# A linear attention and a feed-forward layer on one core: the turn of batch 2's queries behind the load of its values, and the work around tile 0's second layer placed anew

## The chip, the core and the metric

The kernel runs on one core of a Trainium2 chip. The metric is the device time of one execution in microseconds (us); a time given for a kernel is the median of several executions. The engines are named as the profile names them: PE multiplies matrices (PEld is its loading of weights), DVE is the vector engine, ACT the scalar engine, POOL and SP issue most of the transfers (DMAs). PE writes its results to banks of the memory PSUM; all other tiles lie in SBUF.

## The reference

Eight batches of eight heads, 576 rows of 64 numbers each, are put through attention without a softmax; the heads of a row are joined to 512 numbers, and the 4608 rows go through a layer of 2048 hidden units.

```python
kv  = einsum('bhsd,bhse->bhde', k, v)
out = einsum('bhsd,bhde->bhse', q, kv)
rms = sqrt(mean(out * out, axis=-1, keepdims=True) + 1e-06)
x   = (out / rms * g_norm)          # heads joined: [4608, 512]
h   = x @ w_in                      # [512, 2048]
g   = h * (1 / (1 + exp(-1.702 * h)))
y   = g @ w_out                     # [2048, 512]
```

## The kernel before

The rows are worked off in nine tiles of 512: tile t holds the first 512 rows of batch t, and tile 8 the 64 rows that each batch leaves over. A tile has a first layer (h and its gate) and a second layer (the product with w_out). Tile 0 multiplies plainly: 64 products of 128x512 in the first layer (`first_columns`, L473) and 64 in the second (`project_all`, L819). From tile 1 on both layers use seven block products in place of eight (`SevenIn`, L584, and `Seven`, L704), which need sums of blocks: of w_in (`w_in_sums`, L495 to L498), of w_out (`weight_sum`, L612, into `tw`), of the tile's x (`Sums.form`, L512) and of the gated units (`Seven.sums`, L636).

While PE works on a tile, the attention of the next batches is pushed in between. This order is written out by hand: `at1(i, ...)` puts a unit of work behind step i of a tile's first layer, `at2(n, ...)` behind product n of its second. For a batch the units are `kv` (products of k and v into the PSUM tile `kvp`, L259 or L247, then copies into `kvb` or `kvd`), `out` (products with the turned q, L302, and squares on ACT, L320), `ss` (a product with ones, L379, and the reciprocal root on ACT, L381) and `apply` (outT times rs into xT, DVE, L393). From batch 2 on `rows` (L332), `add_up`, `roots` and `turn` stand in their place, and the queries are turned by a transposing DMA from SP (`transpose_q`, L290, into `qTd`; `transpose_rest`, L294, into `qTr`).

Every engine works its own list in order and waits for semaphores, and so do the queues from which DMAs are issued. Nearly all loads are issued by POOL, in one list: batch 0's q, k, v, w_in, then w_out between batch 1's q, k, v (`early_load`, L91; the last pieces of k and v hold the channels of heads 4 to 7), then batch 2's q (`load_q`), and its k and v (`load_kv`, L115, with L120 for the rows left over), which go into the buffers that batch 1's k and v lay in. w_in comes in pieces: hidden blocks 0 to 3 in four pieces of 128 rows, with blocks 8 and 9 ahead of the fourth, then the others; tile 0's hidden blocks are computed in the order `COLS`, which begins 0, 1, 2, 3, 8, 9.

At the start `busy(n)` lets PE multiply zeros n times (128x512, into a bank that nobody reads, L867): 12 before the first turn of q, and 2 in each of two later places.

PSUM has three rings of banks: `ps_a` (three, tag att), `ps_h` (three, tag hT) and `ps_o` (two). A new tile of a ring waits until the readers of the tile three (or two) before it have ended.

Of the kernel before, what the change touches and what calls it, by code (L numbers as in the profile page):

```python
# [16 lines left out]
def kernel(  # L17
# [10 lines left out]
    nc = tc.nc  # L28

    B, H, S, D = q.shape  # L30
# [47 lines left out]
    HF, HN = FO // 2, DM // 2  # L78
# [8 lines left out]
    def early_src(n, b, c0, c1):  # L87
        return srcs[n][b, 2 * c0 : 2 * c1].rearrange("h (p j) d -> p h (j d)", j=NJ)

    def early_load(n, b, c0, c1):  # L90
        nc.gpsimd.dma_start(  # L91
            out=raw[n][0:PE_, c0:c1, :].rearrange("p c (l x) -> p (c l) x", l=2),
            in_=early_src(n, b, c0, c1),
        )
# [13 lines left out]
    kv_rows = {n: raw[n].rearrange("p c x -> p (c x)") for n in "kv"}  # L108
    RW = J * D
    RS = H * RW  # L110
# [26 lines left out]
    def q_rows(b):  # L137

        rows = qbuf if b % 2 else qraw.rearrange("p c x -> p (c x)")
        return rows[:, 0 : H * J * D]  # L140
# [14 lines left out]
    for n in "kqv":  # L155
# [11 lines left out]
        out=ident,  # L167
        in_=ident,
# [36 lines left out]
    def load_w_out(f0, f1):  # L205
        nc.gpsimd.dma_start(
            out=w_out_sb[:, f0:f1, :],
            in_=moe_w_out[f0 * P : f1 * P, :].rearrange("(fo ki) n -> ki fo n", ki=P),
        )
# [11 lines left out]
    class Attention:  # L221
        ss_pool = rest_pool = (ps_a, "att")
# [62 lines left out]
                    r = slice(hl * D, (hl + 1) * D)  # L285
                    copy(self.engine, self.kb[to, c0:c1, half, 1 - hl], self.kvp[r, c0:c1, :])

        def transpose_q(self):
            self.qTd = attn.tile([P, H * J // 2, P], F16, name="qTd", tag="qTd", bufs=1)
            nc.sync.dma_start_transpose(out=self.qTd, in_=q_rows(self.b))  # L290

        def transpose_rest(self):
# [123 lines left out]
    class First(Early):  # L416


        ss_pool = (ps_o, "o")
# [23 lines left out]
    class Second(Early):  # L443


        ss_pool = rest_pool = (ps_h, "hT")
# [82 lines left out]
    def copy(engine, to, src):  # L529
        (nc.vector.tensor_copy if engine == "D" else nc.scalar.copy)(to, src)  # L530
# [280 lines left out]
    def project_all(gT, units):  # L811

        os = {}

        def project(mo, fo):
            if fo == 0:
                pool, tag = (ps_h, "hT") if mo < 2 else (ps_o, "o")
                os[mo] = pool.tile([P, DM], F32, name="o", tag=tag)
            nc.tensor.matmul(  # L819
                os[mo],  # L820
                gT[:, fo, mo * P : (mo + 1) * P],
                w_out_sb[:, fo, :],
                start=(fo == 0),
                stop=(fo == FO - 1),
            )
            if fo == FO - 1:
                copy = nc.scalar.copy if mo % 2 else nc.vector.tensor_copy
                copy(osbs[0][:, mo, :], os[mo])

        steps = [(mo, 4 * i + k) for i in range(3) for mo in range(4) for k in range(4)]  # L830
        steps += [(mo, f + k) for f in (12, 14) for mo in range(2) for k in range(2)]
        steps += [(mo, 12 + k) for mo in (2, 3) for k in range(4)]
        for n, (mo, fo) in enumerate(steps):
            project(mo, fo)
            for u in units.get(n, ()):
                u()
# [28 lines left out]
    def busy(n):  # L865
        for _ in range(n):
            nc.tensor.matmul(  # L867
                idle_ps,
                kvb[1][:, 0, :],
                kvb[1].rearrange("p c r -> p (c r)"),  # L870
                start=True,
                stop=True,
            )
# [15 lines left out]
    a0.ss(0)  # L889
    a0.out(1)  # L890
    a0.q(2)
    a0.kv(2)
    a0.ss(1)
    a0.apply(0)
# [1 line left out]
    a0.q(3)  # L896
    a0.apply(1)
    d0 = Hidden(0)
    a0.kv(3)
    a0.ss(2)  # L900
    a0.apply(2)
# [22 lines left out]
    load_w_out(8, 10)  # L924
    load_w_out(10, 12)
    early_load("v", 1, 0, 2)
    load_w_out(12, 14)
    early_load("k", 1, 2, NPAIR)
    early_load("v", 1, 2, NPAIR)
    load_w_out(14, FO)  # L930

    made = {}
# [44 lines left out]
    live = {0: a0}  # L977
# [4 lines left out]
    for t in range(NT):  # L982
        b = t + 1
        u1, u2 = {}, {}

        def at1(i, f, *args):
            u1.setdefault(i, []).append(lambda: f(*args))

        def at2(i, f, *args):
            u2.setdefault(i, []).append(lambda: f(*args))  # L990

        def of(b, name, *args):
            return lambda: getattr(live[b], name)(*args)

        if t == 0:
            for l in range(2):
                at1(6, nc.vector.memset, kvd[l], 0.0)
            at1(7, of(0, "out", NPAIR))
            at1(7, scale_w_in, 0, 4)
            at1(7, w_in_sums, 0, 2)  # L1000
            at1(8, start, 1)
            at1(12, scale_w_in, 4, 6)
            at1(12, w_in_sums, 2, 3)
            at1(13, load_q, 2)
            at2(4, setattr, a0, "ss_pool", Attention.ss_pool)
            at2(4, of(0, "ss", NPAIR, True))
            at2(4, of(0, "apply", NPAIR))
            at2(18, weight_sum, 0, 0, HF)
            at2(18, scale_w_in, 6, 8)
            at2(18, w_in_sums, 3, 4)  # L1010
            for c in range(NPAIR):
                at1(12, of(1, "pack_q", c))
                at2(9 + 3 * c, of(1, "q", c))
                at2((36, 36, 49, 49)[c], of(1, "kv", c))
                at2((41, 43, 54, 55)[c], of(1, "out", c))
                at2((45, 50, 58, 60)[c], of(1, "ss", c))
                at2((48, 52, 58, 62)[c], of(1, "apply", c))
            for n in range(1, 4):
                at2(19, weight_sum, n, 0, 4)
                at2(38, weight_sum, n, 4, 6)  # L1020
            at2(39, load_kv, 2, 0, H // 2, False)
            at2(51, clear_rest)
            at2(51, load_kv, 2, H // 2, H)

            def first_sum():
                made[1] = Sums(1, xT[1])
                made[1].form(0)

            at2(55, first_sum)
        elif b < B:  # L1030
            todo = plan(t)
            at = todo.attn
            if t == 1:
                at1(todo.steps.index("kv"), of(b, "kv_all", "D"))
                at1(5, start, b)
                at1(5, of(b, "transpose_q"))
                at1(5, of(b, "transpose_rest"))
                at1(4, nc.scalar.preload_act_table_set, "gelu_apprx_sigmoid_and_others")
                for n, i in ((1, 8), (2, 11), (3, 16)):
                    at1(i, weight_sum, n, 6, HF)  # L1040
                at1(22, load_kv, 3)
                at1(22, load_q, 3)
                at2(88, start, 3)
                at2(88, of(3, "kv_all", "A"))
                at2(89, load_kv, 4)
                at2(89, load_q, 4)
            elif t + 2 < B:
                at2(at["rows"][0], start, t + 2)
                at2(at["rows"][0], of(t + 2, "kv_products"))
                at2(52, of(t + 2, "kv_copies", "A"))  # L1050
                if t + 3 < B:
                    at2(at["rows"][0], load_kv, t + 3, 0, H, False, "k")
                    at2(101, after_turn, b)
                    at2(101, load_kv, t + 3, 0, H, True, "v")
                    at2(101, after_queries, t + 2)
                    at2(101, load_q, t + 3)
            if t + 2 < B:
                at2(49 if t > 1 else 100, of(t + 2, "transpose_q"))
                at2(100, of(t + 2, "transpose_rest"))
            at2(at["table"], nc.scalar.preload_act_table_set, "abs_reciprocal_sqrt_and_small")  # L1060
            for h in range(2):
                at2(at["roots"][h], of(b, "roots", h))
            for j in range(J):
                if j < J // 2:
                    at2(at["rows"][j], of(b, "rows", j))
                for name in ("add_up", "turn"):
                    at2(at[name][j], of(b, name, j))
            rest = (80, 90, 96, 97) if 1 < t < B - 2 else (46, 74, 80, 82)
            at2(rest[0], of(b, "out", NPAIR))
            at2(rest[1], of(b, "ss", NPAIR))  # L1070
            at2(rest[2], of(b, "apply", NPAIR))
            at2(rest[3], nc.scalar.preload_act_table_set, "gelu_apprx_sigmoid_and_others")
        elif t < B:
            for name in ("ss_pool", "rest_pool"):
                at2(16, setattr, live[1], name, (ps_a, "att"))
            at2(16, of(1, "out", NPAIR))
            at2(34, nc.scalar.preload_act_table_set, "abs_reciprocal_sqrt_and_small")
            at2(44, of(1, "ss", NPAIR))
            at2(50, of(1, "apply", NPAIR))
            at2(52, nc.scalar.preload_act_table_set, "gelu_apprx_sigmoid_and_others")  # L1080
        layers(t, u1, u2)
# [30 lines left out]
```

## Time and profile before

| | |
|---|---|
| median of 3 runs | 259.14 us (258.35, 259.14, 259.88) |
| the profiled execution, its own time | 259.74 us |
| its span, from first to last instruction | 258.0 us |
| PE busy | 251.7 us (98%) |
| DVE, ACT, POOL busy | 193.9, 177.1, 57.0 us |
| mean granted clock of PE | 0.993 |

The profile is of one execution. A window is a stretch of the span in us from its start; `PEclk` is the share of the full clock that PE was granted in it. In a row of the timeline the first number is the start, the second the time until the last of the group has ended; what ended an idle time stands in brackets. For a DMA the row of the queue gives when it was issued, and the row of the issues how long it took from issue to landing.

### The profile page before, as it was taken

How to read it: one execution, taken by the hardware profiler on the slowest of the kernel's cores; microseconds unless marked ns; L12 is line 12 of the kernel's file. 1: busy time of each engine (PE TensorE's matmuls, PEld its weight loads, DVE VectorE, ACT ScalarE, POOL GpSimd, SP SyncE). 2: the span in 40 equal slices, each digit the busy share in tenths (PEclk: the TensorE clock that was granted, in tenths of full speed). 3: DMA queues.
4: the chain of work that ended last, by engine and by line, in shares of the span. 5: the costliest groups of instructions: out<-in, count | busy, mean ns of one | idle time of the engine just before them, and what ended most of it. 6: DMA issues, size and time to landing. Idle time of an engine off the chain costs nothing.

```text
span 258.0 us, 6355 instructions
## 1 busy us (share of the span) xinstructions
PE 251.7 (98%) x2596; PEld 204.4 (79%) x2596; DVE 193.9 (75%) x344; ACT 177.1 (69%) x322; POOL 57.0 (22%) x92
## 2 busy tenths in 40 slices
PE   8899999999999999999999999999999999999994
PEld 2444454788888888888888888898888888888883
DVE  1546685899958986798679867987799787857872
ACT  3458743988758894899579957995799469536800
POOL 8773244208061013301150134000000000000013
PEclk9979999999999999999999999999999999999999
DMA  7999999999989979996999699909500430012005
GB/s 181 194 188 206 204 204 197 216 216 115 184 159 208 221 91 224 153 158 81 186 184 164 84 205 135 190 5 136 202 4 0 84 163 3 0 57 108 3 19 145
DMA packets 68687, 35.33 MB, mean 137 GB/s; under 512 B 37970, under 2 KB 66258, under 8 KB 68402
## 3 DMA queue, kind: packets, MB, share of 16 engines
q0 software_dynamic: 37632, 18.31, 55.3%
q1 hardware_dynamic: 30624, 16.29, 27.4%
q8 instruction: 20, 0.33, 0.5%
q10 hardware_dynamic: 402, 0.33, 0.5%
q14 instruction: 9, 0.07, 0.1%
HBM read 36.70 MB, written 9.44 MB: 179 GB/s over the span
## 4 chain that ended last, share of the span: by engine, by line
PE 93%; DMA 4%; issue 0%; POOL 0%; DVE 0%
PE o L704 38%; PE h L584 38%; PE hT L473 6%; PE o L819 5%; DMA vbuf<-in_v_dram 2%; DMA qraw<-in_q_dram 2%; PE kvp L247 2%; PE outR L332 1%; PE ss L379 1%; PE outT L302 1%; PE q L454 0%; PE kvp L259 0%; PE outT L306 0%; PE kv L259 0%; DVE osb L684 0%
## 5 line engine op out<-in xcount | busy, mean ns | idle before, releaser
L561 ACT ACTIVATE gT<-h 128x512 f16<-128x512 f32 x96 | 52.5, 601 | 5.6 <-PE h L584 5.6
L584 PEld LDWEIGHTS <-ws 128*128 128x128 f16 x512 | 50.1, 98 | 5.9
L704 PEld LDWEIGHTS <-gS 128*128 128x128 f16 x512 | 49.1, 98 | 6.1 <-DVE gS L636 0.3
L584 PE MATMUL h<-xS,ws 128*128 128x256 f16 x384 | 52.2, 273 | 0.0
L704 PE MATMUL o<-tw,gS 128*128 128x256 f16 x384 | 45.6, 273 | 0.0
L584 PEld LDWEIGHTS <-w_in_sb 128*128 128x128 f16 x384 | 37.4, 98 | 4.7
L704 PEld LDWEIGHTS <-gT 128*128 128x128 f16 x384 | 37.6, 98 | 4.3
L704 PE MATMUL o<-w_out_sb,gT 128*128 128x256 f16 x256 | 31.4, 273 | 0.0
L584 PE MATMUL h<-xT,w_in_sb 128*128 128x256 f16 x224 | 31.1, 272 | 0.0
L681 DVE TENSOR_TENSOR osb<-o,qf 128x512 f32<-128x512 f32 (+1 forms) x25 | 16.7, 669 | 11.7 <-PE o L704 11.7
L598 DVE TENSOR_TENSOR h<-h,s 128x512 f32<-128x512 f32 x32 | 22.2, 698 | 4.2 <-PE h L584 2.6
L600 DVE TENSOR_TENSOR s<-h,s 128x512 f32<-128x512 f32 x32 | 22.1, 691 | 4.1 <-PE h L584 3.3
L738 POOL DMA_DIRECT2D out_dram<-osb x6 | 3.2, 537 | 93.2 <-DVE osb L681 93.2
L636 DVE TENSOR_TENSOR gS<-gT 128x512 f16<-128x512 f16 (+2 forms) x32 | 21.3, 685 | 0.6 <-ACT gT L561 0.6
L561 ACT ACTIVATE gT<-s 128x512 f16<-128x512 f32 x32 | 19.8, 628 | 2.4 <-DVE s L600 2.3
L530 DVE COPY s<-h 128x512 f32<-128x512 f32 x19 | 13.0, 686 | 8.2 <-PE h L584 8.2
L584 PE MATMUL h<-xS,w_in_sb 128*128 128x256 f16 x128 | 18.9, 273 | 0.0
L115 POOL DMA_DIRECT2D kraw<-in_k_dram x7 | 6.0, 853 | 56.9 <-PE kvp L247 52.0
L348 DVE TENSOR_REDUCE sum<-sq 128x8 f32<-128x512 f16 x24 | 14.9, 678 | 4.7 <-ACT sq L342 4.7
L320 ACT ACTIVATE sq<-outT 128x512 f16<-128x512 f32 (+1 forms) x16 | 7.9, 495 | 15.1 <-PE outT L302 9.5
L990 ACT ACT_TABLE_LOAD x14 | 18.0, 1283 | 0.2
L381 ACT ACTIVATE rs<-ss,eps_t 128x512 f32<-128x512 f32 (+1 forms) x16 | 9.2, 582 | 12.4 <-PE ss L379 12.3
(104 smaller groups left out, 373.9 us busy)
## 6 DMA issues: line engine op xcount, KB each, us to landing
out_dram<-osb SPq DMA_DIRECT2D x8, 512.0 KB, 4.6
kraw<-in_k_dram POOLq DMA_DIRECT2D x5, 512.0 KB, 6.0
vbuf<-in_v_dram POOLq DMA_DIRECT2D x5, 512.0 KB, 10.4
out_dram<-osb SPq DMA_DIRECT2D x2, 1024.0 KB, 4.9
qraw<-in_q_dram POOLq DMA_DIRECT2D x3, 512.0 KB, 11.6
qbuf<-in_q_dram POOLq DMA_DIRECT2D x3, 512.0 KB, 10.4
out_dram<-osb SPq DMA_DIRECT2D x6, 192.0 KB, 5.9
w_in_sb<-in_moe_w_in_dram POOLq DMA_DIRECT2D x2, 512.0 KB, 10.1
```

Source lines behind the costliest of these rows:

```text
L348: nc.vector.tensor_reduce(out=self.sum4[:, j, :], in_=self.o[j][1].rearrange("p (x d) -> p x d", d=D), op=ALU.add, axis=mybir.AxisListType.X,)
L473: nc.tensor.matmul(self.h[fo], w_in_sb[:, ko, fo * P : (fo + 1) * P], self.x[:, ko], start=(ko == 0), stop=(ko == KO - 1),)
L530: (nc.vector.tensor_copy if engine == "D" else nc.scalar.copy)(to, src)
L561: nc.scalar.activation(self.gT[:, to, n * TH : (n + 1) * TH], src, AFT.Gelu_apprx_sigmoid)
L584: nc.tensor.matmul(bank[name][:, a], w, x, start=(p in (1, 5) and a == 0 and k == 0), stop=(k == KH - 1), skip_group_check=True,)
L598: nc.vector.tensor_add(bank["z"], bank["x"], self.s5)
L600: nc.vector.tensor_add(self.s5, bank["x"], self.s5)
L636: op(s[:, n, lo], a, b)
L681: nc.vector.tensor_add(o, ps, self.kept[with_][:, m])
L704: nc.tensor.matmul(o, a, w, start=(p in (1, 2, 5) and i == 0 and (mo == 0 or split)), stop=(i == HF - 1), skip_group_check=True,)
L819: nc.tensor.matmul(os[mo], gT[:, fo, mo * P : (mo + 1) * P], w_out_sb[:, fo, :], start=(fo == 0), stop=(fo == FO - 1),)
L990: u2.setdefault(i, []).append(lambda: f(*args))
```

## The change

Six edits. (1) `busy(1)` stands between the turn of batch 0's third pair of heads and its kv, and `busy(2)` before the fourth pair's kv: three products of zeros more. (2) In POOL's list the load of w_out's blocks 12 and 13 is cut in two and goes behind the last pieces of batch 1's k and v. (3) The last 16 products of tile 0's second layer run through the four row blocks for hidden block 12, then for 13, then two each for 14 and 15, in place of groups of two row blocks. (4) Batch 1's kv, out, ss and apply stand behind other products of that layer, the two halves of batch 2's k and v are loaded at 41 and 54 in place of 39 and 51, and the last `ss` takes its bank from `ps_a`. (5) The sums of w_out's blocks 4 and 5 (n = 1 to 3) leave tile 0; they are formed together with blocks 6 and 7 in tile 1, n = 1 and 2 in its first layer, n = 3 behind product 80 of its second. (6) Before batch 2's queries are turned, POOL copies one number of the last row of v's rest into `qTd`, so that the copy waits for that load, and SP's transposing DMA waits for the copy.

```diff
-        def transpose_q(self):
+        def transpose_q(self, after=None):
             self.qTd = attn.tile([P, H * J // 2, P], F16, name="qTd", tag="qTd", bufs=1)
+            if after is not None:
+                nc.gpsimd.tensor_copy(out=self.qTd[0:1, 0, 0:1], in_=after)
             nc.sync.dma_start_transpose(out=self.qTd, in_=q_rows(self.b))
...
         steps = [(mo, 4 * i + k) for i in range(3) for mo in range(4) for k in range(4)]
-        steps += [(mo, f + k) for f in (12, 14) for mo in range(2) for k in range(2)]
-        steps += [(mo, 12 + k) for mo in (2, 3) for k in range(4)]
+        steps += [(mo, fo) for fo in (12, 13) for mo in range(4)]
+        steps += [(mo, 14 + k) for mo in range(4) for k in range(2)]
...
     a0.q(2)
+    busy(1)
     a0.kv(2)
...
     d0 = Hidden(0)
+    busy(2)
     a0.kv(3)
...
     early_load("v", 1, 0, 2)
-    load_w_out(12, 14)
     early_load("k", 1, 2, NPAIR)
     early_load("v", 1, 2, NPAIR)
+    load_w_out(12, 13)
+    load_w_out(13, 14)
     load_w_out(14, FO)
...
             at2(4, setattr, a0, "ss_pool", Attention.ss_pool)
+            at2(57, lambda: setattr(live[1], "ss_pool", Attention.ss_pool))
...
-                at2((36, 36, 49, 49)[c], of(1, "kv", c))
-                at2((41, 43, 54, 55)[c], of(1, "out", c))
-                at2((45, 50, 58, 60)[c], of(1, "ss", c))
-                at2((48, 52, 58, 62)[c], of(1, "apply", c))
+                at2((40, 40, 47, 47)[c], of(1, "kv", c))
+                at2((44, 45, 51, 54)[c], of(1, "out", c))
+                at2((47, 48, 56, 58)[c], of(1, "ss", c))
+                at2((50, 52, 57, 60)[c], of(1, "apply", c))
             for n in range(1, 4):
                 at2(19, weight_sum, n, 0, 4)
-                at2(38, weight_sum, n, 4, 6)
-            at2(39, load_kv, 2, 0, H // 2, False)
-            at2(51, clear_rest)
-            at2(51, load_kv, 2, H // 2, H)
+            at2(41, load_kv, 2, 0, H // 2, False)
+            at2(54, clear_rest)
+            at2(54, load_kv, 2, H // 2, H)
...
-                at1(5, of(b, "transpose_q"))
+                at1(5, of(b, "transpose_q", kv_rows["v"][0:1, RS + H * D - 1 : RS + H * D]))
...
-                for n, i in ((1, 8), (2, 11), (3, 16)):
-                    at1(i, weight_sum, n, 6, HF)
+                for n, i in ((1, 8), (2, 11)):
+                    at1(i, weight_sum, n, 4, HF)
+                at2(80, weight_sum, 3, 4, HF)
```

## The prediction

> **What bounds the kernel now.** I read the page first (busy times, clock slices, chain), then the windows around the one dip of the clock, then PE's timeline there.
>
> ```profile
> PE 251.7 (98%) x2596; PEld 204.4 (79%) x2596; DVE 193.9 (75%) x344; ACT 177.1 (69%) x322; POOL 57.0 (22%) x92
> PEclk9979999999999999999999999999999999999999
> PE 93%; DMA 4%; issue 0%; POOL 0%; DVE 0%
> ```
>
> The chain is PE for 93% of the span, and a DMA for the 4% at the start: until 13.3 us PE waits for batch 0, and from there to the last product it never waits long. A step off PE gains nothing unless PE waits for it; only the number of PE's products, their clock, and PE's waits set the end. The change removes no product and adds three. The one slice in which the clock is low is the third, and here it is by windows:
>
> ```profile
> core 0: us, PE busy (x) PEld busy (x) DVE busy (x) ACT busy (x) POOL busy (x), PEclk, DMA share, GB/s
> 6.55:9.96 3.41, 3.03 (x59) 1.77 (x58) 1.73 (x6) 0.60 (x1) 2.38 (x5) 1.00 1.28 191
> 9.96:13.37 3.41, 2.50 (x45) 1.31 (x46) 2.32 (x7) 2.35 (x4) 2.96 (x5) 1.00 1.28 196
> 13.37:16.79 3.42, 3.42 (x20) 1.50 (x20) 1.45 (x3) 1.28 (x2) 3.16 (x5) 0.50 1.30 179
> 16.79:20.20 3.41, 3.41 (x18) 1.51 (x17) 1.72 (x3) 1.99 (x3) 1.96 (x3) 1.00 1.30 204
> ...
> 252.30:255.70 3.40, 1.99 (x19) 1.54 (x16) 1.27 (x3) 0.00 (x0) 1.60 (x4) 1.00 0.73 185
> ...
> 254.00:258.00 4.00, 0.29 (x3) 0.01 (x1) 0.42 (x1) 0.00 (x0) 0.00 (x0) 1.00 0.49 125
> ```
>
> A stretch of 3.42 us has half the clock, with PE busy all through it: 1.7 us of products are lost. Ahead of it lies a stretch with PE busy for 2.50 us of 3.41. Yet 1.99 busy us at the end (252.3 to 255.7) did not lower the clock behind them (254 to 258 has 1.00). So busy time alone isn't what the gate counts: the stretch that lost the clock is full of small products, the one that kept it of full ones.
>
> ```profile
> 12.17 0.45 PE L434 MATMUL q<-ident,qraw 96*64 96x96 f16 x12
> 13.29 0.50 PE L259 MATMUL kv<-vbuf,kraw 96*64 96x64 f16 x12 [0.68 <-DMA vbuf<-in_v_dram]
> ...
> 17.17 2.11 PE L473 MATMUL hT<-xT,w_in_sb 128*128 128x512 f16 x9
> 17.34 5.61 PE hT L473 x26
> ```
>
> The last row is from the chain: 5.61 / 26 = 0.216 us for a 128x512 product at full clock.
>
> **The change part by part.** *Three idle products and the clock.* They cost 3 x 0.216 = 0.65 us of PE. All stand ahead of the 0.68 us in which PE waits for v (row of 13.29), so I take 0 while v lands where it does, and 0.65 at worst. They bring 0.65 us of full products into the stretch from 9.96 to 13.37, which then has some 3.1 busy us, about the 3.03 of the stretch before it, which kept the clock. I take it that the clock stays: -1.7 us from the products, with 0 as the other end.
>
> The Trainium skill, "TensorE: Matmul & The Clock Gate" (section "Why this matters for your kernels"), lets the clock drop after a whole window of idle PE and warns of gaps over some 3 us; by that rule there would be no dip here and nothing to gain, a sum of +0.2 us. The trace disagrees: its widest gap there is 0.68 us, and the clock fell. The same page (section "Part 4: PE-mode transpose") says that transposes do not count as busy to the gate; by that rule the idle products matter more than their share of busy time. The two windows of 2.50 and 1.99 us bear this out.
>
> *What is late next.* PE, 1.7 us ahead at 16.8, comes to hidden block 8, whose w_in is a load of its own:
>
> ```profile
> 10.50 1.28 POOL L180 DMA_DIRECT2D w_in_sb<-in_moe_w_in_dram  x2 [0.21 <-issue]
> ...
> w_in_sb<-in_moe_w_in_dram POOLq DMA_DIRECT2D x1, 256.0 KB, 7.0
> ```
>
> The first of these two, blocks 8 and 9, is issued at 10.50 and lands at 17.5. The nine products from 17.17 on are the last two of the second quarter of blocks 0 to 3, the four of the third, and then block 8's: that begins at 17.17 + 6 x 0.216 = 18.47 before and would at 16.77 after. With 0.1 us from landing to product PE goes on at 17.6, so +0.8 us is given back, in this execution's state of the loads. If they landed 0.8 us sooner it would be 0; I keep both ends. Net so far -0.9, or -1.7.
>
> *Batch 1's steps and the order of the last 16 products.* Same products, so only new waits count.
>
> ```profile
> 41.92 0.38 PE L379 MATMUL ss<-sq,ones 128*128 128x512 f16 x1
> 42.33 0.69 ACT L381 ACTIVATE rs<-ss,eps_t 128x512 f32<-128x512 f32 x1
> 43.05 0.69 DVE L393 TENSOR_TENSOR xT<-outT,rs 128x512 f16<-128x512 f32 x1 [1.69 <-ACT rs L381]
> 43.09 0.57 PE L259 MATMUL kvp<-vbuf,kraw 96*64 96x64 f16 x24
> 43.70 0.59 DVE L408 CAST kvb<-kvp 64x128 f16<-64x128 f32 x2
> ```
>
> The third `out` takes the bank of the first, which `apply` of the first must have left. Before, six products and the kv lay between. Now: ss, 24 small products (0.50 us without the drain), then ss and four products to `out`: 0.22 + 0.50 + 0.22 + 4 x 0.216 = 1.8 us after ss began. DVE meanwhile has the two copies into kvb (from 0.76 to 1.35 us) and only then apply (to 2.04). So PE waits some 0.3 us. The shorter distance from the first kv to `out` (four products, 0.86 us, where the copies alone take 0.59) may add 0.1, and small waits of this layer that now go, 0.2 together, come off. I take +0.2 us, with -0.2 and +0.6 as ends.
>
> *w_out's later load.* k and v go ahead of 256 KB.
>
> ```profile
> 30.14 0.67 POOL L91 DMA_DIRECT2D vbuf<-in_v_dram  x1 [1.92 <-DMA qraw<-in_q_dram]
> ...
> vbuf<-in_v_dram POOLq DMA_DIRECT2D x1, 288.0 KB, 11.9
> ...
> 30.00:40.00 10.00, 10.00 (x89) 5.23 (x88) 7.35 (x17) 4.91 (x7) 3.71 (x6) 1.00 1.28 203
> ```
>
> v's last piece lands at 42.0 before; at 203 GB/s 256 KB are 1.3 us, so it lands at 40.7. Its kv at 43.09 moves up by two products (0.43) and the gain (0.9), to 41.8: covered by 1.1 us, of which nothing is left if the gain is 1.7 and the loads a little late. Blocks 12 and 13 land at about 41.4 and 42.0, first needed behind product 47, at about 42: covered by a few tenths. 0, at worst +0.5.
>
> *w_out's sums later.*
>
> ```profile
> 37.72 0.69 DVE L612 TENSOR_TENSOR tw<-w_out_sb,tw 128x1024 f16<-128x1024 f16 x1
> 40.26 0.42 DVE L612 TENSOR_TENSOR tw<-w_out_sb,tw 128x512 f16<-128x512 f16 x1
> 48.00:58.00 10.00, 10.00 (x126) 8.75 (x125) 9.60 (x20) 9.01 (x17) 0.00 (x0) 1.00 1.25 223
> 73.39 1.91 PE L704 MATMUL o<-tw,gT 128*128 128x256 f16 x16
> 73.59 0.69 DVE L681 TENSOR_TENSOR osb<-o,qf 128x512 f32<-128x512 f32 x1 [1.51 <-PE o L704]
> ```
>
> Tile 0 loses 3 x 0.42 = 1.26 us of DVE. Tile 1's first layer has two of 0.69 (twice the 512 numbers) for three of 0.42: +0.12 us in a stretch where DVE has 0.4 us idle in 10. The third falls behind product 80, into the 1.51 us in which DVE waits before 73.59, ahead of the product that reads it (73.39). 0, with 0.2 either way.
>
> *The turn of batch 2's q.* POOL's copy (its like below takes 0.18 us) has behind it in POOL's list only batch 3's loads, which wait for the same batch's kv anyway; behind SP's transpose stand the turn of the rest and, later, xT's.
>
> ```profile
> 46.35 0.69 POOL L120 DMA_DIRECT2D vbuf<-in_v_dram  x1 [0.41 <-DMA qrem<-in_q_dram]
> vbuf<-in_v_dram POOLq DMA_DIRECT2D x1, 64.0 KB, 9.5
> 51.40 4.26 SPq L290 DMA_TRANSPOSE qTd<-qraw  x1
> qTd<-qraw SPq DMA_TRANSPOSE x1, 6.4
> 57.10 0.28 PE L247 MATMUL kvp<-vbuf,kraw 128*64 128x64 f16 x6
> 63.26 0.32 PE L332 MATMUL outR<-kvd,qTd 64*128 64x64 f16 x10
> 100.30 0.18 POOL L127 COPY mark<-xT 1x1 f16<-1x1 f16 x1 [9.10 <-DMA xT<-x]
> ```
>
> v's rest lands at 46.35 + 9.5 = 55.85, 1.25 us before its kv at 57.10. That product moves to 56.4, so v is in time even if the turn's going brings it no sooner; a gain of 1.7 would need it 0.5 us sooner, and that is what the wait may buy. The turn is then issued at about 56.1 and lands, with the 6.4 us it took here, at 62.5; `rows` reads it at 63.26 - 0.7 = 62.6. Covered, by 0.1 us: 0.
>
> **Sum.** -1.7 + 0.8 + 0.2 = -0.7 us: 259.74 - 0.7 = 259.0 for a profiled execution, whose own time is 0.6 us above the median of 259.14. Taken off that median: **258.4 us**.
>
> **The rivals.** *A, the forecast* (0.38): 258.4.
>
> *B, the loads come sooner than in the profiled execution* (0.34). The whole 1.7 us then shows, and the waits of tile 0's second layer go the good way: 259.14 - 1.7 + 0.1 = 257.5. For it: the three runs lie 1.5 us apart, about what the dip costs, so waits and dip vary from run to run, and v's earlier landing fits a PE that is 1.7 us ahead. Against: the load of blocks 8 and 9 does not depend on the change, and in the trace it lands at 17.5.
>
> *C, the idle products do not do what they are for* (0.12): the dip stays, or in most runs there was none to remove. With the sum of the rest 259.14 + 0.2 = 259.3. For it: the run of 258.35 may be one without a dip. Against: the dip in the trace follows just the stretch that is filled.
>
> The same page of the Trainium skill (section "What's actually happening") calls the gate's window free-running, which would shift it between runs; one trace can't show that.
>
> *D, slower: the turn is late* (0.16). The point is 62.6 us: every us by which `qTd` lands later is a us of PE, at `rows`. The turn now runs beside batch 3's k and v, which POOL issues as soon as kv has ended, and which it preceded before. If they take half of the transfers from it, the 4.26 us of its issue become 8.5, it lands at 64.7 or later, and the price is 2.1 us: 260.5. Against: it has some two us before the first of these loads moves data.
>
> **How the numbers follow.** 0.5% of 259.14 is 1.3 us, about what a measurement of this kernel can tell from no change: the bounds are 257.84 and 260.44. B lies beyond the first; of A, 0.03 where the loads give back little. Faster: 0.37. Slower: D, 0.16. Same: 0.35 of A and C's 0.12, 0.47. The range goes from 257.3 (B with all its ends) to 260.2 (C with the ends of the layer's and the sums' waits, and most of D's way); left out are the late half of D and the edge of B.
>
> **What would show it.** PEclk 1.00 through 13.4 to 16.8; PE waiting at about 16.8 to 17.6 for w_in_sb; a wait of some 0.3 us for a bank near 42.5; kv of batch 2 near 56.4 without a wait; SP's turn issued at about 56 and landing before `rows` near 62.6. A dip that is still there, or a wait of a us or more at L334 (the old L332) for qTd, would make the prediction wrong.

## The result, and the profile after

The changed kernel takes 260.45 us (median of 22 executions, 259.07 to 262.82) against 259.51 us of the kernel before (22 executions, 258.33 to 260.54): 1.0053 times as long, 95% interval 1.0035 to 1.007. The forecast was 258.4. The profiled execution of the changed kernel took 260.2 us, its span is 258.4 us. Medians here are over all executions; the ratios leave out those that lie more than 1.5% above the fastest of the same kernel.

The page of the changed kernel: PE's busy time, the clock in 40 slices, and the chain.

```profile
PE 250.2 (97%) x2599; PEld 203.6 (79%) x2599; DVE 194.0 (75%) x341; ACT 177.0 (68%) x322; POOL 57.9 (22%) x94
...
PEclk9999999999999999999999999999999999999999
...
PE 67%; DMA 19%; POOL 6%; issue 5%; DVE 1%; DVEq 0%; POOLq 0%
```

The dip is gone, and PE is busy for 1.5 us less although it has three products more. Yet the span is 0.4 us longer: the chain, 93% PE before, now runs through transfers for 19%. The windows at the old dip (columns as before: PE, PEld, DVE, ACT, POOL, clock, DMA share, GB/s):

```profile
9.96:13.37 3.41, 3.27 (x55) 1.58 (x54) 2.17 (x6) 2.35 (x4) 2.99 (x6) 1.00 1.27 192
13.37:16.79 3.42, 3.42 (x27) 1.38 (x21) 1.87 (x4) 2.38 (x4) 2.95 (x4) 1.00 1.35 195
```

The list of PE's waits (total us, times, longest) has three behind the start (from 15 us on) that the kernel before did not have:

```profile
PE kvp L247 <- DMA vbuf<-in_v_dram: 1.1, 1, 1.1
...
PE outR L334 <- DMA qTd<-qraw: 0.4, 1, 0.4
PE hT L475 <- DMA w_in_sb<-in_moe_w_in_dram: 0.3, 1, 0.3
```

Where they stand, in PE's timeline:

```profile
42.20 0.38 PE L381 MATMUL ss<-sq,ones 128*128 128x512 f16 x1
...
55.87 0.82 PE L247 MATMUL kvp<-vbuf,kraw 128*64 128x64 f16 x40
...
62.48 0.64 PE L334 MATMUL outR<-kvd,qTd 64*128 64x64 f16 x32 [0.38 <-DMA qTd<-qraw]
...
88.36 0.32 PE L247 MATMUL kvp<-vbuf,kraw 128*64 128x64 f16 x8
89.73 0.70 PE L247 MATMUL kvp<-vbuf,kraw 128*64 128x64 f16 x32 [1.05 <-DMA vbuf<-in_v_dram]
90.36 0.64 PE L334 MATMUL outR<-kvd,qTd 64*128 64x64 f16 x32
```

The same place in the kernel before, where batch 4's kv runs through without a wait:

```profile
89.21 0.82 PE L247 MATMUL kvp<-vbuf,kraw 128*64 128x64 f16 x40
89.97 0.64 PE L332 MATMUL outR<-kvd,qTd 64*128 64x64 f16 x32
```

Read together, the two timelines show where the profiled execution loses what it had won. PE is 1.23 us ahead at batch 2's kv (55.87 against 57.10), 0.85 us ahead at batch 4's kv (88.36 against 89.21), and 0.39 us behind once that kv is done (90.36 against 89.97). The last figure is the 0.4 us by which the span is longer.

The wait at 62.5 is that of batch 2's `rows` for the turn. The one at 89.7, the largest, is in batch 4's kv: its first 8 products run, the ninth needs v's last 64 rows, which come late. The queues behind both, SP's and then POOL's (start, time to issue):

```profile
55.96 1.73 SPq L292 DMA_TRANSPOSE qTd<-qraw  x1
...
67.94 4.57 SPq L370 DMA_TRANSPOSE xT<-x  x2
72.67 4.71 SPq L292 DMA_TRANSPOSE qTd<-qbuf  x1
...
78.91 8.54 SPq L845 DMA_DIRECT2D out_dram<-osb  x8
```

```profile
55.76 0.18 POOL L291 COPY qTd<-vbuf 1x1 f16<-1x1 f16 x1 [9.12 <-DMA vbuf<-in_v_dram]
56.97 0.89 POOL L115 DMA_DIRECT2D kraw<-in_k_dram  x1 [1.03 <-PE kvp L247]
...
72.10 0.90 POOL L115 DMA_DIRECT2D kraw<-in_k_dram  x1 [9.39 <-PE kvp L247]
```

Two numbers decide what follows. The turn's **lead** is the time from its issue to the issue of batch 3's k, here 56.97 - 55.96 = 1.0 us. And batch 3's own turn (`qTd<-qbuf`) took 4.71 us to issue, where before it took 1.92, and tile 1's stores behind it were issued at 78.9 instead of 76.1. The rows of the kernel before:

```profile
72.17 1.92 SPq L290 DMA_TRANSPOSE qTd<-qbuf  x1
...
76.10 6.13 SPq L843 DMA_DIRECT2D out_dram<-osb  x8
```

### The profile page after: what moved, and what is told of

Same layout as the page of the kernel before. It is cut to its first block, busy times and chain, and to the rows that moved or that the text cites. A ratio compares the mean times of both kernels' runs of the same rounds, so it can differ in the third digit from the quotient of the medians.

```text
span 258.4 us, 6362 instructions
## 1 busy us (share of the span) xinstructions
PE 250.2 (97%) x2599; PEld 203.6 (79%) x2599; DVE 194.0 (75%) x341; ACT 177.0 (68%) x322; POOL 57.9 (22%) x94
## 4 chain that ended last, share of the span: by engine, by line
PE 67%; DMA 19%; POOL 6%; issue 5%; DVE 1%; DVEq 0%; POOLq 0%
PE o L706 36%; PE h L586 28%; DMA w_out_sb<-in_moe_w_out_dram 6%; DMA vbuf<-in_v_dram 6%; DMA qraw<-in_q_dram 4%; DMA qTd<-qraw 2%; POOL w_in_sb L180 2%; PE kvp L247 1%; PE outR L334 1%; POOL qraw L91 1%; POOL kraw L91 1%; POOL vbuf L91 1%; DVE tw L614 0%; POOL vbuf L115 0%; DVE w_in_sb L219 0%
## 5 line engine op out<-in xcount | busy, mean ns | idle before, releaser
L532 ACT COPY h<-h 128x512 f32<-128x512 f32 x27 | 15.4, 577 | 2.2 <-PE h L586 1.9
L586 PE MATMUL h<-xT,ws 128*128 128x256 f16 x112 | 16.8, 272 | 0.0
```

The costliest lines, as they stand in the source:

```text
L586: nc.tensor.matmul(bank[name][:, a], w, x, start=(p in (1, 5) and a == 0 and k == 0), stop=(k == KH - 1), skip_group_check=True,)
```

## The experiments

Three theories were written down. T (transfers): the turn, put beside batch 3's loads, pushes all transfers behind it later, until batch 4's v is late. L (layer): the new order of tile 0's second layer and of the loads costs. N: the dip is not there in most executions, so that its removal wins nothing. A fourth, D2, came after the first four runs: it is the turn's own landing that varies. Each group of kernels ran on one chip beside the kernel before, whose median was 258.9 to 259.1 us there.

**One part at a time.** e1, the wait taken out:

```diff
-                at1(5, of(b, "transpose_q", kv_rows["v"][0:1, RS + H * D - 1 : RS + H * D]))
+                at1(5, of(b, "transpose_q"))
```

> The changed kernel without the wait of batch 2's turn; all else as changed. Theory T (transfers): the waiting turn moves from 50-57 us to 56-62 us, beside batch 3's k and v, and all transfers behind them land later, so that PE waits 0.43 us at rows and 1.24 us at batch 4's kv (89.7). Without it the wait at rows goes and that at batch 4's kv falls below 0.6 us, though batch 2's kv may wait up to 0.4 us: about 259.4 us against 260.5, that is 0.4% below the changed kernel. Theory L (layer): the new order in tile 0's second layer and of the loads costs the time, the turn only its 0.43 us: 260.0. Theory N (no dip in most runs, so that the idle products have nothing to win): 260.0 to 260.5, with batch 4's kv still waiting about 1 us.

Measured: 258.68 us, 0.9988 (0.9973 to 1.0002). The loss is gone, and with it the waits at `rows` and at batch 4's kv. SP's timeline and the landing (last column, us from issue):

```profile
52.44 3.09 SPq L292 DMA_TRANSPOSE qTd<-qraw  x1
...
71.24 1.66 SPq L292 DMA_TRANSPOSE qTd<-qbuf  x1
...
75.15 6.83 SPq L845 DMA_DIRECT2D out_dram<-osb  x8
```

```profile
qTd<-qraw SPq DMA_TRANSPOSE x1, 5.2
```

The turn is issued 4.7 us ahead of batch 3's k (57.15); batch 3's turn is issued in 1.66 us instead of 4.71, and tile 1's stores 3.8 us sooner.

e2, the kernel before with the three idle products alone:

```diff
+    busy(1)
     a0.kv(2)
...
+    busy(2)
     a0.kv(3)
```

> The kernel before with only the 3 idle products added. Theory T: the dip at 13.4 to 16.8 us goes (-1.7 us), w_in gives back 0.4, and batch 2's and batch 4's kv, which have no slack in the kernel before, give back some 0.3 each: 258.8 us against 259.5. Theory L: nothing is given back at the transfers: 258.2. Theory N: 259.5, unchanged within 0.2 us.

Measured: 258.81 us, 0.9998 (0.9976 to 1.0021): nothing, as N has it (T's 258.8 was reckoned against 259.5 for the kernel before, which took 258.9 here). Its profile, with the clock at 1.00 throughout, shows batch 2's kv waiting for its v:

```profile
56.44 0.69 PE L247 MATMUL kvp<-vbuf,kraw 128*64 128x64 f16 x32 [0.77 <-DMA vbuf<-in_v_dram]
```

e3 takes the idle products out of the changed kernel (the diff above, reversed).

> The changed kernel without the 3 idle products. The dip should be back at 13.4 to 16.8 us in the profile. Theory T: PE comes to batch 2's rows and batch 4's kv 1.3 us later, so the waits there (0.43 and 1.24 us) nearly go, and the time is that of the changed kernel: 260.3 us. Theory L: 1.3 us more than the changed kernel, 261.7. Theory N: no dip in most runs with or without them: 260.4, but then batch 4's kv keeps its wait of about 1.2 us.

Measured: 259.69 us, 1.0028 (1.0007 to 1.005). The dip at 13.4 us is not back, though PE is as little busy ahead of it as in the kernel before: that speaks for N. (In e4 below, which has no idle products either, PE is busy for 2.52 us of that stretch, and its profile has no dip.) But its profile (an execution of 262.1 us) shows the turn at its worst: windows, waits, then SP's, POOL's and the landing's rows.

```profile
9.96:13.37 3.41, 2.46 (x52) 1.46 (x52) 2.65 (x6) 1.96 (x4) 3.18 (x5) 1.00 1.29 202
13.37:16.79 3.42, 3.29 (x16) 1.38 (x16) 1.62 (x3) 2.75 (x4) 2.63 (x4) 1.00 1.37 197
```

```profile
PE outR L334 <- DMA qTd<-qraw: 2.9, 1, 2.9
```

```profile
55.41 2.97 SPq L292 DMA_TRANSPOSE qTd<-qraw  x1
```

```profile
56.52 0.89 POOL L115 DMA_DIRECT2D kraw<-in_k_dram  x1 [1.13 <-PE kvp L247]
```

```profile
qTd<-qraw SPq DMA_TRANSPOSE x1, 9.0
```

With a lead of 1.1 us the turn took 9.0 us, and PE waited 2.9 us for it.

e4, the wait alone, in the kernel before (the turn's lines of the change and nothing else).

> The kernel before with only the wait of batch 2's turn added. Theory T: the turn is issued at 56 us, lands at 62.5 and is covered at rows (63.3), but batch 4's v lands some 0.5 to 1 us later, and its kv, which has no slack at 89.2, waits that long: 260.2 us against 259.5. Theory L: nothing late, 259.5. Theory N says nothing of it: 259.5 to 259.9.

Measured: 259.83 us, 1.0027 (1.0008 to 1.0046): the wait costs by itself, and the time is what T has. The wait to which T puts it down is not seen here: the profiled execution (259.4 us, below its median) had a lead of 57.78 - 56.31 = 1.5 us, a landing of 5.4 us and no wait of either kind, so it doesn't show the cost.

e11, the wait and the idle products without the layer:

> The kernel before with the 3 idle products and the turn's wait, and without the new order of loads, steps and sums: the change less its layer. If the layer is worth nothing (the kernels with and without it stood at 258.7 and 258.8 where the turn didn't wait): as the changed kernel, 259.7. If the layer brings v sooner and so hides part of the turn's wait: 260.2 or more, since batch 2's v then lands at 56.4 (0.7 later than with the layer), and with it the turn; if the layer costs: 259.2.

Measured: 259.89 us, 1.0028 (1.0002 to 1.0054); its profile has the wait at batch 4's kv:

```profile
PE kvp L247 <- DMA vbuf<-in_v_dram: 0.8, 1, 0.8
```

So the wait costs with and without the layer, and of the layer, as long as the turn does not wait, e1 against e2 (0.9988, 0.9998) shows no cost: L falls.

**When the turn is issued.** e5 is the changed kernel again, on the chip of e6 to e8.

> The changed kernel as it is, as the mark for the runs beside it: 1.0053 of the kernel before, as measured, about 260.3 us if the kernel before takes 258.9. Theory D2 (the turn's own landing, 5.2 to 9.0 us after its issue in the profiles so far, decides: issued at 56, it lands anywhere from 61 to 65, and rows wants it at 62.0): the runs spread by 3 us, the longest with the clock at 0.99, since a wait of almost 3 us at rows is followed by a dip. Theory T (batch 4's v): a wait of about a us at batch 4's kv in most runs, a spread of 1 us.

Measured: 259.76 us, 1.004 (1.0014 to 1.0066), 259.06 to 263.54; the profile again has the wait at batch 4's kv, and batch 3's turn issued slowly. PE's waits, then SP:

```profile
PE kvp L247 <- DMA vbuf<-in_v_dram: 1.2, 1, 1.2
```

```profile
72.18 5.15 SPq L292 DMA_TRANSPOSE qTd<-qbuf  x1
```

e6 lets the turn wait for an earlier piece of v:

```diff
-                at1(5, of(b, "transpose_q", kv_rows["v"][0:1, RS + H * D - 1 : RS + H * D]))
+                at1(5, of(b, "transpose_q", kv_rows["v"][0:1, RS - 1 : RS]))
```

> The changed kernel, but the turn waits for the second half of batch 2's v (landing about 53.5 us) rather than for its last 64 rows (55.7). The turn's issue is then near 53.6, between the 52.4 without the wait and the 56.0 of the change. Theory D2: it lands before 62 even when it takes 8 us, so nothing waits at rows: 258.8 us, the time without the wait (0.999 of the kernel before). Theory T: two thirds of the delay of batch 3's loads are gone: 259.2. If it is the wait itself that costs, wherever it ends (POOL held up, one instruction more): 260.3, as the changed kernel.

Measured: 258.93 us, 1.0005 (0.9984 to 1.0025). The same copy and the same kind of wait, 1.4 us earlier than in e5 beside it (54.12 against 55.50), and the loss is gone, so neither the copy nor the wait costs by itself:

```profile
54.12 1.79 SPq L292 DMA_TRANSPOSE qTd<-qraw  x1
```

e10 puts it off the other way, until the copies of batch 2's kv:

```diff
-                at1(5, of(b, "transpose_q", kv_rows["v"][0:1, RS + H * D - 1 : RS + H * D]))
...
+                at1(22, of(b, "transpose_q", kvd[b % 2][D : D + 1, NPAIR - 1, 1, 0, D - 1 : D]))
                 at1(22, load_kv, 3)
```

> The changed kernel with the turn put off further: it waits for the copies of batch 2's kv (about 57.7 us) instead of for its v (55.7), just ahead of batch 3's loads. Theory D2: it lands 5.2 to 9 us behind its issue, at 63 to 67, where PE wants it at 62: waits of 1 to 5 us at rows in every run, with a dip of the clock behind them where they are some 2.5 us or more: 261 to 263 us, clocks of 0.99 in most runs; batch 4's kv no longer waits, since PE comes late to it. Theory T alone: no step at rows, 260.2 to 260.7.

Measured: 267.9 us, 1.0337 (1.0302 to 1.0373), beyond even what D2 gave: the turn was issued at 59.5 in place of 58 and took 10.2 us. SP, POOL, landing, PE's waits:

```profile
59.45 2.80 SPq L292 DMA_TRANSPOSE qTd<-qraw  x1
```

```profile
59.36 0.88 POOL L115 DMA_DIRECT2D kraw<-in_k_dram  x1
```

```profile
qTd<-qraw SPq DMA_TRANSPOSE x1, 10.2
```

```profile
PE outR L334 <- DMA qTd<-qraw: 7.4, 1, 7.4
```

**What stands beside it.** e7 makes batch 3's loads light:

```diff
-                at1(22, load_kv, 3)
+                at1(22, load_kv, 3, 0, 1)
```

> The changed kernel, with one of the 8 heads of batch 3's k and v loaded and the other 7 left as batch 2's (a part of the loads left out): 0.9 MB less to move between 57 and 68 us, right behind the turn's issue. Theory D2 with the cause in the contention with these loads: the turn lands 5.2 us or less behind its issue, by 61.2, rows does not wait, batch 4's v comes in time, and the time is 258.6 us. If the turn's long landing is its own (or that of stores and of the turn of the rest): rows still waits 0 to 3 us, 259.5 or more, with clocks of 0.99 in some runs. Theory T alone: rows' 0.4 us stays, batch 4's wait goes: 259.2.

Measured: 259.4 us, 1.002 (1.0003 to 1.0037). By the medians about half of the loss is gone, though the interval overlaps that of e5 (1.0014 to 1.0066), and of the long executions none is left (none of twelve above 260.2; of e5, three took 261.6 or more). With a lead of only 0.9 us the turn landed in 6.0 us, and neither `rows` nor batch 4's kv waited in the profile. That the median did not fall to 258.6 is unexplained.

e12 leaves the loads whole and holds them back with ten tiny copies on POOL ahead of `load_kv`, which read batch 2's finished kv.

> The changed kernel with batch 3's loads held on POOL until batch 2's kv is copied and ten tiny copies are done, to about 59 us instead of 57, so that the turn, issued at 56, has a lead of 3 us instead of 1. Theory D2 (the turn against batch 3's loads): the turn lands in 5.2 to 6 us, rows waits at most a few tenths, no run has a clock of 0.99, and the median falls below the changed kernel's by 0.3 to 0.8 us. Theory T (batch 4's v): everything behind lands another 1 to 2 us later, so that batch 4's kv, or batch 3's kv, waits more than 1.2 us: the median rises by 0.5 to 1.5 us.

Measured: 266.85 us, 1.0255 (1.0211 to 1.0298). The copies took 4.67 us, more than twice what I had reckoned, so that the loads came at 63.8 and not at 59. The landing shows what it was meant to show, and PE's waits what it cost:

```profile
qTd<-qraw SPq DMA_TRANSPOSE x1, 5.0
```

```profile
PE kvp L247 <- DMA vbuf<-in_v_dram: 6.4, 3, 3.8
```

Free of batch 3's loads the turn lands in 5.0 us, the shortest of all, and `rows` does not wait; batch 3's kv waits 6 us instead, for its loads. The time itself tells nothing between the theories.

e9 moves batch 4's kv, the one that waits at 89.7, behind step 32 of tile 2's second layer:

```diff
-                at2(at["rows"][0], start, t + 2)
-                at2(at["rows"][0], of(t + 2, "kv_products"))
+                i = 32 if t == 2 else at["rows"][0]
+                at2(i, start, t + 2)
+                at2(i, of(t + 2, "kv_products"))
...
-                    at2(at["rows"][0], load_kv, t + 3, 0, H, False, "k")
+                    at2(i, load_kv, t + 3, 0, H, False, "k")
```

> The changed kernel with the products of batch 4's kv 17 steps (1.9 us of PE) later in tile 2, behind step 32 instead of 15; the turn still waits. Theory T: v's last rows land at 89.2 to 89.7, PE now comes to the kv at about 90, so the wait of 1.1 to 1.2 us that both profiles of the changed kernel show there is gone, and the median falls by 0.8 to 1.1 us: 258.8 to 259.0. The longest runs, with a wait at batch 2's rows, stay. Theory D2 (rows alone): no change, 259.7.

Measured: a median of 262.22 us, 258.96 to 265.23; 1.003 (0.9986 to 1.0074). Inconclusive: seven of its twelve executions took 261.9 or more, and the profiled one (262.5 us) waited 2.7 us at `rows`, upstream of the edit (turn issued at 57.21, batch 3's k at 57.96, landing 8.4 us). It was run again, e13, with the changed kernel, e14, beside it.

> The kernel of e9 again: batch 4's kv 1.9 us of PE later. Theory T: below the changed kernel beside it by 0.8 us, the long runs staying. Theory D2: as the changed kernel.

> The changed kernel, the mark for the two beside it: 1.004 to 1.005 of the kernel before, some 259.9 to 260.4 us; a profile with a wait of about 1.2 us at batch 4's kv, or with one of 2.5 us or more at batch 2's rows.

Measured: e14 261.09 us, 1.0075 (1.0043 to 1.0107), more than expected; e13 259.44 us, 1.0012 (0.9979 to 1.0045). Both fall into two groups. Of e14 five executions took 259.7 to 261.1 and four 262.3 to 263.9; of e13 seven took 258.8 to 259.5 and five 262.3 to 263.5. The lower group is what the edit moves, by 1.7 us between the groups' medians (260.82 to 259.09), back to the kernel before; the two lower groups do not overlap. That is more than the 1.1 to 1.2 us of the wait in the profiles, and the rest is not explained. The upper group stays. e13's kv in its new place, without a wait:

```profile
90.95 0.82 PE L247 MATMUL kvp<-vbuf,kraw 128*64 128x64 f16 x40
```

And e14's profile, an execution of the upper group: PE's waits, and the clock behind the wait.

```profile
PE outR L334 <- DMA qTd<-qraw: 2.7, 1, 2.7
```

```profile
65.00:66.00 1.00, 1.00 (x32) 0.85 (x27) 0.01 (x1) 0.64 (x2) 0.00 (x0) 0.50 1.58 185
66.00:67.00 1.00, 1.00 (x7) 0.69 (x6) 1.00 (x2) 1.00 (x3) 0.00 (x0) 0.50 1.42 191
```

A wait of 2.7 us ends at 64.75, and the clock behind it is at half speed: this execution pays for both. The half clock does not always follow. The profile of e9 has a wait at `rows` of the same length (2.7 us, ending at 65.75), and the clock behind it stayed whole:

```profile
66.00:67.00 1.00, 1.00 (x34) 0.88 (x27) 0.20 (x1) 0.82 (x2) 0.00 (x0) 1.00 1.49 196
```

What the three profiles of executions above 262 us with the turn in its place (e3, e9, e14) share is the wait of 2.7 to 2.9 us at `rows`.

e8 was meant to beat both kernels: e1 with the load of w_in's blocks 8 and 9 split.

```diff
-    load_w_in(8, 10)
+    load_w_in(8, 9)
+    load_w_in(9, 10)
```

> A version meant to beat both: the changed kernel without the turn's wait, and with the load of w_in's blocks 8 and 9 split into one for each block. PE waited 0.5 us for it at 17.3. If block 8 lands 0.6 us sooner and block 9 is in time for its products (0.65 us later): 258.3 us, 0.9975 of the kernel before. If rows of 256 bytes make the two loads slower than the one, or the one issue more (0.65 us of POOL) puts w_out's loads off to where they are late: 258.7 to 259.2.

Measured: 258.66 us, 0.9991 (0.9976 to 1.0006). Its profile has no wait for w_in, but the time is that of e1: neither is shown to beat the kernel before.

**The turn's lead and its landing**, from the profiles of all kernels in which the turn waits (lead: batch 3's k issue minus the turn's issue):

| kernel | turn issued | lead, us | landing, us | wait at `rows` | wait at batch 4's kv |
|---|---|---|---|---|---|
| e10 | 59.45 | -0.1 | 10.2 | 7.4 | 0 |
| e9 | 57.21 | 0.8 | 8.4 | 2.7 | kv moved |
| e14 (changed) | 56.00 | 0.9 | 8.6 | 2.7 | 0 |
| the change | 55.96 | 1.0 | 6.4 | 0.4 | 1.1 |
| e3 | 55.41 | 1.1 | 9.0 | 2.9 | 0 |
| e5 (changed) | 55.50 | 1.2 | 5.6 | 0 | 1.2 |
| e13 | 55.97 | 1.4 | 5.6 | 0 | kv moved |
| e4 | 56.31 | 1.5 | 5.4 | 0 | 0 |
| e11 | 55.65 | 1.5 | 5.6 | 0 | 0.8 |
| e6 | 54.12 | 2.4 | 6.0 | 0 | 0 |
| e12 | 56.40 | 7.4 | 5.0 | 0 | 0 |

(e7, its loads light, stands apart: lead 0.9, landing 6.0.) Below a lead of some 1.2 us the turn takes 8.4 us or more in four of five profiles; above it 5 to 6. The waiting turn starts when v's last rows land, and batch 3's loads start when batch 2's kv, which needs the same rows, has ended: where the turn waits for these rows and the loads are not held back, the lead is at most 1.5 us. Batch 3's loads are not the only traffic that counts: in e2, where the turn does not wait and is issued at 49.51, it took 8.1 us, beside loads of batch 2 that were still under way.

## Why the prediction was wrong

**The clock, -1.7 us: the term is that of the profile, not of the kernel.** The dip at 13.4 us went as forecast in the profile. But of 113 executions of the kernel before on four chips, 99 have a mean clock of 0.997 or more, and only 14 one of 0.993 or less; the profiled one (0.993) was of the few. (The clocks of the 22 executions beside the result are not on record, nor where the others of the 14 lost theirs.) On two of the chips these few were 0.6 to 0.7 us longer than the median of the rest, on the other two 1.5 to 1.6. In the median there was next to nothing to win: e2, 0.9998. My rival C ("in most runs there was none to remove") was right for this term; I had read "2.50 busy us ahead of it", with the small products and transposes in it, as the cause; e3 and e4 have the same transposes there, 2.46 and 2.52 busy us, and no dip. What sets off the dip stays open.

**The wait for w_in, +0.8.** It is 0.4 us in the profile (block 8's product at 17.15, where 15.44 + 6 x 0.216 = 16.74 was possible; the list of waits puts 0.3 of it down to the load). It stands in e4 too (0.5 us, without idle products) and is missing in e2 (with them): it varies with the landing of that load, and is not shown to be a cost of the change.

**Tile 0's second layer, +0.2; w_out's load and sums, 0.** Right within what can be told. The third `out` (43.06) did not wait; a gap of 0.1 us stands ahead of it, before the ss at 42.20 (41.86 plus one product of 0.216 to 42.20), and none of 0.3. From its first product to tile 1's first the layer takes 18.0 us before and after (29.81 to 47.80, 28.51 to 46.52), so the term came to nothing. No wait for w_out or its sums shows. The layer's new places may still shorten the lead: it is 1.5 us in the profiles of e4 and e11, without them, and 0.8 to 1.4 in the six with them (the changed kernel three times, e3, e9, e13). Of 24 executions of the first two, one took 261.5 us or more, of 79 of the others 25. That was not separated further.

**The turn, 0: this step failed.** Batch 2's kv moved to 55.87 (56.4 forecast) without a wait; the turn was issued at 55.96 and landed at 62.3, as forecast. What was wrong is, first, that one duration (6.4 us) stood for all. It runs from 5.0 to 10.2 us, and a cover of 0.1 us is none. I named the mechanism as rival D, with its place and a price of 2.1 us, and argued against it that the turn has "some two us" before batch 3's loads move data; the lead is half that. D's time, 260.5, is the one measured, but by coincidence: D has 2.1 us at `rows`, and the profiled execution waits 0.4 us there and 1.1 us at batch 4's kv, which D does not have. Where the turn is in time (e4, e11), the median is high all the same.

Second, I named what stands behind the transpose in SP's queue and costed none of it. Batch 3's loads land later, though they are issued sooner (its q takes 11.0 us to land, 9.2 before), and run into xT's transposes (4.57 us to issue, 3.26 before); batch 3's turn is then issued at 72.67, behind batch 4's k (72.10), and is stretched in its turn; tile 1's stores come 2.8 us later and share the engines with batch 4's v. The other profiles agree with the middle step. In the four in which batch 3's turn is issued 0.3 us or more behind batch 4's k (the change, e5, e11, e12) it takes 4.7 to 5.5 us to issue, in the twelve others 1.7 to 3.1. The first three of the four are also the only ones with a wait at batch 4's kv. What v's last rows of batch 4 do, by their issue (with its ns and start) and the time to landing, in the kernel before and in the changed one:

```profile
L120 POOL DMA_DIRECT2D vbuf<-in_v_dram x1: 723/723/723, 75.4 to 75.4; - x1
...
DMA to landing us min/median/max: 13.9/13.9/13.9
```

```profile
L120 POOL DMA_DIRECT2D vbuf<-in_v_dram x1: 713/713/713, 74.5 to 74.5; - x1
...
DMA to landing us min/median/max: 15.2/15.2/15.2
```

Before, they landed at 75.4 + 13.9 = 89.3, when their kv (89.21) had just begun: there was no slack at all. Now they are issued 0.9 us sooner and land at 89.7, while PE comes 0.85 us sooner, at 88.36. e1 undoes the delay and takes the whole loss away; e13 moves the reader and takes that of its lower group away. So the wait at 89.7 is shown to be a part of the loss. The steps in between are read from the traces, and only their two ends were tested.

So the changed kernel's executions are of two sorts: those with 0.8 to 1.2 us at batch 4's kv, and those in which the turn landed late, with some 2.7 us at `rows` and in most of them a clock lost behind it. Of 43 executions 12 took 261.5 us or more, ten of these with a mean clock of 0.993 or less, against 1 of 113 of the kernel before; that all 12 had the wait at `rows` is inferred from the profiles of three such executions (e3, e9, e14).

## What to carry to other kernels

Before a stretch of a trace is priced as a gain, ask in how many executions it is there: the mean clock of every run tells that where one profile cannot. A transfer that is made to wait for another does not only start later: it is moved beside whatever that other's landing also sets off, so work out its lead over those loads, and follow the queue behind it to the next reader without slack, even 30 us on. A landing time is to be taken from the traffic that will be beside it, not from the traffic that was.

## What had not been expected of the hardware

A transposing DMA of 512 KB from SP landed in 5.0 us with no load beside it (e12), and in 5.2 to 10.2 us beside loads from POOL's queue; it was 8.4 us and more in four of the five profiles in which whole loads were issued less than 1.2 us behind it. The Trainium skill, "DMA: Bandwidth & Descriptors" (section "Queues, rings and completion order"), says that each transfer engine goes round the queues that have work, packet by packet; sharing of that kind agrees with the doubled time (5.0 to 10.2). Why half a microsecond of lead makes so much of a difference, the runs do not show.

The clock fell to 0.50 behind waits of PE of 2.7 us (e14) and 2.9 us (e3), and not behind one of 2.7 us in e9. The Trainium skill, "TensorE: Matmul & The Clock Gate" (section "Why this matters for your kernels"), asks for no gaps over some 3 us; here a slightly shorter one sufficed, in two of three profiles. The same page (section "What's actually happening") calls the gate's window free-running. That like waits, and the like stretch at 10 to 13 us, lose the clock in some executions and not in others is what such a window would give; the runs show only that it varies.
